# A list scheduler inside the program orders every engine between attention and the last stage; weights are kept as fp32 or as words

## The chip, the cores and the metric

One core of a Trainium2 chip. The time is the device time of one launch, in microseconds; three runs of the kernel before are known, and one execution was recorded by the hardware profiler. PE is the matrix engine; DVE (VectorE), ACT (ScalarE) and POOL (GpSimd) do everything elementwise; SP issues the transfers, all but two small ones at the start.

## The reference

```python
# attention: retention with a decay mask, 4 batches x 8 heads, 576 positions, head width 64
ret = scores * Dmat[None, :, :, :]              # scores = q k^T / sqrt(D), Dmat = gamma^(i-j), lower triangle
x = ret @ v                                     # -> 2304 tokens x 512
# first MLP, 512 -> 2048 -> 512
h = x @ w_in
g = h * np.clip(h + 3.0, 0.0, 6.0) / 6.0
x = g @ w_out
# second MLP, 512 -> 1024 -> 512
h = x @ w_in
e = np.exp(h - h_max)
sm = e / (np.sum(e, axis=-1, keepdims=True) + 1e-09)
solu = h * sm
ln = (solu - mu) / np.sqrt(var + 1e-06) * g_ln
out = ln @ w_out
```

## The kernel before, in words

Every large product is made of three PE passes over numbers split into a high and a low word (hi x hi, hi x lo, lo x hi), so each operand exists as two words: ACT copies the value to the high word, and DVE or POOL subtracts to get the low one. The weights arrive as 64-bit numbers. `Weights.value` (lines 134 to 150) turns half a weight tile, 512 KB, into fp32: ACT reads both 32-bit halves of the raw tile `wraw` (L140, L145), DVE shifts and adds (L148, L149). `wraw`, `wz` and `wt` have two buffers each. `words` (L152) splits the result.

The 2304 tokens are five blocks, 0 to 3 of 512 and 4 of 256. The first MLP has 16 slices of its inner width. After attention come: x2 (the second product) of block 0 over slices 0 to 5 in turns with h (the first product and the gate) of block 1 (`mlp_turns`, L342); h of block 4 and x2 of block 1 over these slices; x2 of block 4. The rest is done by `paired` (L462), which takes two blocks and a list of pairs of slices. For each pair `seven` (L389) makes the seven products of a Strassen-like scheme (a, b, c, d accumulate in four PSUM banks; `plus` adds them, `gate` makes r on ACT and the gated value on DVE), and x2 units of the first block run between the products (`next(units)`). The second block's gated values wait in `later` and are split one by one (`split_g`) while its x2 units run. `paired` is run three times: blocks 0, 1 with pairs 3 to 7; blocks 2, 3 with pairs 0 to 2; blocks 2, 3 with pairs 3 to 7, with `h_4` (L443) for block 4 beside it. The forms of x for `seven` come from `x_sums` (L510), those of the weights from `in_pair` (L196), which converts two halves and makes sums and splits into four `wi` buffers (six there are). `out_half` (L187) converts the second weights, splits them, and stores them to `w1s` in DRAM; `load_out` brings them back. `w2_halves` (L224) does the same for the second MLP's weights.

Conversions stand in one list, `todo` (L891 to 899), taken up by `wq.step()` from hooks at fixed points of the PE's work. Pairs 3 to 7 are in it twice, and pairs 0 to 2 are there although their slices were converted and split in `w1_halves` (L171) during attention.

What sets the order: attention's PE and ACT instructions are kept in program order, and the last stage is pinned wholly (`Pinned`, L60) by a hand-written list of events with times. Between them nothing is pinned: the framework's own timeline model decides, when the program is built, in which order each engine gets its instructions, and also SP its transfers. On the chip each engine and SP's queue then work in that order.

## Time and profile before

| | us |
|---|---|
| median of 3 runs | 729.58 (728.76 to 733.24) |
| the profiled execution | 728.7 |
| its span, first to last instruction | 726.8 |
| PE busy | 662.1 |
| DVE, ACT, POOL busy | 475.5, 421.5, 391.0 |
| mean granted clock of PE, of full speed | 0.948 |

The span counts from the first to the last instruction. PE's busy time also counts the time by which a matmul is longer at the lower of PE's two clock levels (1.2 instead of 2.4 GHz), so it is compared with the time its matmuls need at full clock. The granted clock is an average over a stretch, as a share of full speed. A wait is put down to what released it last.

### The profile page before, as it was taken

The page shows a single profiled execution, that of the slowest core. Times are in us where ns is not written, and L with a number is a line of the kernel's source. Part 1 is how long each engine was busy: PE and PEld are TensorE (multiplying, and loading weights), DVE is VectorE, ACT ScalarE, POOL GpSimd, SP SyncE. Part 2 cuts the span into 40 slices and gives each one's busy share as a digit, 9 for nine tenths or more (in the row PEclk, how much of TensorE's full clock was granted, in tenths as well). Part 3 has the DMA queues.
Part 4 walks back from the last instruction along what each step waited for, and adds up shares of the span by engine and source line. Part 5 has one row for each costly group of instructions (what it writes and reads, how often), then busy time and mean ns, then how long its engine had stood idle before and what let it go on. Part 6 is the DMA issues. An engine that isn't in the chain of part 4 may idle for free.

```text
span 726.8 us, 11418 instructions
## 1 busy us (share of the span) xinstructions
PE 662.1 (91%) x4100; PEld 532.4 (73%) x4100; DVE 475.5 (65%) x791; ACT 421.5 (58%) x736; POOL 391.0 (54%) x372
## 2 busy tenths in 40 slices
PE   9999969989998779968848989979999999999998
PEld 6788848867876458846636878857798888888887
DVE  3766796348889984579335778831138887788760
ACT  5887456556556725356453566543036777777773
POOL 4764553414335766224602343367337989999743
PEclk9999989999999769999985999988999999999999
DMA  9999406887356729733693464796467554443343
GB/s 330 387 357 323 145 28 220 296 282 273 120 158 230 259 68 376 267 120 144 196 380 119 117 205 156 273 367 246 139 186 202 151 94 95 113 103 76 88 93 81
DMA packets 91340, 142.85 MB, mean 197 GB/s; under 512 B 43794, under 2 KB 51090, under 8 KB 91284
## 3 DMA queue, kind: packets, MB, share of 16 engines
q1 hardware_dynamic: 91136, 142.11, 60.4%
q8 instruction: 32, 0.52, 0.3%
q14 instruction: 24, 0.20, 0.1%
q10 hardware_dynamic: 148, 0.02, 0.0%
HBM read 95.18 MB, written 37.49 MB: 183 GB/s over the span
## 4 chain that ended last, share of the span: by engine, by line
PE 51%; DVE 21%; DMA 14%; ACT 7%; issue 6%; POOL 1%; SPq 1%; DVEq 0%; ACTq 0%; POOLq 0%
PE o L68 14%; PE h L68 12%; PE acc L323 10%; DMA wraw<-in_w_dram 9%; DVE wz L149 3%; PE h L300 3%; DVE wz L148 2%; PE xp L569 2%; DVE ws L211 2%; PE s L569 2%; PE x L68 2%; DVE t L401 2%; DVE later L381 2%; DMA wraw<-in_w2i_dram 2%; DMA wraw<-in_w2o_dram 2%
## 5 line engine op out<-in xcount | busy, mean ns | idle before, releaser
L323 PE MATMUL acc<-g,w1l 128*128 128x512 f32 x624 | 170.0, 416 | 24.6 <-ACT g L385 7.9
L323 PEld LDWEIGHTS acc<-g,w1l 128*128 128x128 f32 x624 | 123.2, 202 | 62.6 <-ACT g L385 11.1
L68 PE MATMUL o<-w,lt 128*128 128x512 f32 (+1 forms) x456 | 103.0, 378 | 0.0
L148 DVE TENSOR_SCALAR wz<-wz 128x512 int32<-128x512 int32 x60 | 37.1, 618 | 90.8 <-ACT wz L140 90.7
L68 PEld LDWEIGHTS o<-w,lt 128*128 128x128 f32 x456 | 82.4, 188 | 16.3 <-POOL lt L68 0.4
L386 POOL TENSOR_TENSOR g<-gf,g 128x512 fp32r<-128x512 f32 x26 | 39.6, 1528 | 64.4 <-ACT g L385 63.0
L68 POOL TENSOR_TENSOR lt<-lT,lt 128x512 fp32r<-128x512 f32 x36 | 62.3, 1749 | 15.2 <-ACT lt L68 15.2
L140 ACT ACTIVATE wz<-wraw 128x512 f32<-128x512 f32 x60 | 39.8, 664 | 49.3 <-DMA wraw<-in_w_dram 41.0
L68 ACT ACTIVATE e<-h,stat 128x1024 f32<-128x1024 f32 x36 | 41.3, 1148 | 35.3 <-DVE stat L68 35.3
L149 DVE CUSTOM_DVE_ANT_0 wz<-wz,wt 128x1024 uint16<-128x1024 uint16 x60 | 54.5, 908 | 6.9 <-ACT wt L145 1.8
L219 POOL TENSOR_TENSOR w1f_a<-wz,w1f_a 128x512 fp32r<-128x512 f32 (+1 forms) x26 | 31.3, 1203 | 46.7 <-ACT w1f_a L218 30.8
L300 PE MATMUL h<-x,w 128*128 128x512 f32 (+1 forms) x216 | 49.3, 372 | 7.3 <-DVE gf L313 7.1
L68 PE MATMUL h<-w2t,xt 128*128 128x512 f32 x216 | 53.4, 389 | 0.0
L300 PEld LDWEIGHTS h<-x,w 128*128 128x128 f32 x216 | 36.4, 193 | 17.0 <-DVE gf L313 8.4
L219 POOL TENSOR_TENSOR w1f_s<-ws,w1f_s 128x512 fp32r<-128x512 f32 x13 | 18.2, 1403 | 56.6 <-ACT w1f_s L218 48.6
L386 POOL TENSOR_TENSOR g<-later,g 128x512 fp32r<-128x512 f32 x26 | 38.2, 1488 | 15.4 <-ACT g L385 15.3
L68 PEld LDWEIGHTS h<-w2t,xt 128*128 128x128 f32 x216 | 40.3, 188 | 8.2
L145 ACT ACTIVATE wt<-wraw 128x512 int32<-128x512 uint32 x64 | 42.3, 665 | 0.2 <-POOL w1f_s L219 0.2
L395 PE MATMUL sa<-x_b,w1f_a 128*128 128x512 f32 x96 | 30.9, 456 | 11.4 <-ACT w1f_a L218 8.0
L68 PE MATMUL h<-w2b,xt 128*128 128x512 f32 x162 | 39.7, 390 | 0.0
L317 POOL TENSOR_TENSOR g<-gf,g 128x512 fp32r<-128x512 f32 (+1 forms) x18 | 21.7, 1206 | 33.3 <-ACT g L316 33.2
L380 ACT ACTIVATE r<-t,half 128x512 f32<-128x512 f32 x39 | 28.0, 718 | 17.1 <-DVE t L401 15.5
(180 smaller groups left out, 1448.1 us busy)
## 6 DMA issues: line engine op xcount, KB each, us to landing
wraw<-in_w_dram SPq DMA_DIRECT2D x48, 512.0 KB, 5.9
w1l<-w1s SPq DMA_DIRECT2D x34, 512.0 KB, 6.7
w1s<-w1o SPq DMA_DIRECT2D x10, 512.0 KB, 3.7
rv<-in_vt_dram SPq DMA_DIRECT2D x16, 288.0 KB, 5.6
x2l<-x2s SPq DMA_DIRECT2D x18, 256.0 KB, 4.1
x2f<-x2o SPq DMA_DIRECT2D x18, 256.0 KB, 3.6
x2r<-x2f SPq DMA_DIRECT2D x9, 512.0 KB, 4.3
rq<-in_qt_dram SPq DMA_DIRECT2D x13, 352.0 KB, 6.1
```

Source lines behind the costliest of these rows:

```text
L68: return lambda *args, **kw: self.keep(op(*args, **kw))
L140: first = se.activation(out=z.bitcast(F32), in_=raw[:, :, 1].bitcast(F32), func=ACTF.Prelu, scale=2.0 ** -112, alpha=2.0 ** 32)
L145: second = se.activation(out=t, in_=raw[:, :, 0].bitcast(U32), func=ACTF.Copy, scale=2.0 ** -29)
L148: ve.tensor_scalar(out=z, in0=z, scalar1=3, scalar2=None, op0=ALU.logical_shift_left)
L149: ve.tensor_tensor(out=z, in0=z, in1=t, op=ALU.add)
L219: eng.tensor_tensor(out=w[:, 1, c], in0=src[:, c], in1=f32(w[:, 0, c]), op=ALU.subtract)
L300: mm = nc.tensor.matmul(hp, w1t[ff, 0][:, a, c], xb[t, p][:, b, :n], start=(p == 0 and i == 0), stop=(p == NP - 1 and i == 2),)
L323: te.matmul(acc, w1t[ff, 1][:, a, c], g[:, b], start=(first and i == 0), stop=(last and i == 2))
L380: se.activation(out=r, in_=src, func=ACTF.Relu, scale=1.0 / 6.0, bias=half)
L386: ge.tensor_tensor(out=w[:, 1], in0=src, in1=f32(w[:, 0]), op=ALU.subtract)
L395: te.matmul(bank, forms[k][w][:, a, p * 128:(p + 1) * 128], xf[x][p][:, b], start=(first and p == 0 and i == 0), stop=(last and p == 1 and ...
L569: keep(nc.tensor.matmul(*args, **kw))
```

## The change

From attention's end to the last stage the functions no longer issue instructions. They enter operations into a `Plan`: engine, an assumed duration, what is read and written, and a function that issues it. `place` fixes PE's order as the program has it, gives each buffer's next user the buffers in turn, and works a due time back from PE's ideal times. `run` then goes through time: of the operations ready on an engine it takes the one due first; SP's transfers share a modelled rate; an operation entered with `either` runs on POOL, or on DVE when POOL would be late or DVE is free. The instructions are then issued in that order with all engines pinned. The framework places the waits as before.

Beside it: the words of slices 0 to 5, split during attention, are stored (`w1w`), and pairs 0 to 2 load them and add hi and lo ("words"); pairs 3 to 7 are converted once ("new"), their fp32 values stored in `wf` and loaded for the second time ("kept"). PE's order has other turns: the products of a pair in the order 0, 2, 5, 1, 3, 6, 4; block 4's x2 units in the first pair of the first `paired`, three after each product; the second block's last eight units carried into the next `paired`; x2 opens with two slices on one accumulator. The sums that end banks c and d are written back to PSUM. Of `t` there are three buffers instead of four, of `x2l` four instead of two; the pool of attention is released at once. The last stage is the same.

```diff
+    HOP, DMA_US, DMA_KB, DMA_ONE = 0.2, 2.2, 330.0, 150.0
...
+    def op(self, engine, us, fn, reads=(), writes=(), kb=0, slack=0.0, alt=None):
+        o = Op(len(self.ops), engine, us, fn, kb, slack, alt)
...
+        for key in (*reads, *writes):
+            for k in self.related(key):
+                w, r = self.last.setdefault(k, ([], []))
+                o.after.update(w)
+                if key in writes:
+                    o.after.update(r)
+        for key in (*reads, *writes):
+            self.last[key][key not in writes].append(o)
...
+    def lag(self, a, b):
+        same = 0.0 if a.engine == "PE" else 0.03
+        return b.slack + (same if a.engine == b.engine and a.engine != "SP" else self.HOP)
+
+    def length(self, o):
+        return self.DMA_US + o.kb / self.DMA_ONE if o.engine == "SP" else o.us
...
+
+        pe = [o for o in self.ops if o.engine == "PE"]
+        now, ideal = 0.0, {}
+        for a, b in zip(pe, pe[1:]):
+            b.after.add(a)
+        for o in pe:
+            ideal[o] = now
+            now += o.us
...
+                if len(slots) >= bufs:
+                    kept = all(any(o.engine == "PE" for o in v.ops) for v, _ in slots)
+                    free = min(range(len(slots)), key=lambda i: slots[i][1]) if kept else 0
+                    old = slots.pop(free)[0]
+                    b.ops[0].after.update(old.ops)
+                    assert b.ops[0] not in old.ops, (b.name, old.name)
+                if first:
+                    b.ops[0].begun.add(first)
+                first = b.ops[0]
+                slots.append((b, max(asap[o] + self.length(o) for o in b.ops)))
+        order = self.sorted_ops()
...
+            if o in ideal:
+                due = min(due, ideal[o] + o.us)
+            o.due = min(o.due, due - self.length(o))
+            for v in o.begun:
+                v.due = min(v.due, o.due)
...
+                waiting[o.engine].append(o)
+        dma, done = 0.0, []
+
+        def late(o, t):
+            busy = sum(v.us for v in waiting["POOL"] if v.due < o.due and ready[v] <= t)
+            return max(free["POOL"], t) + busy > o.due
+
...
+            if e == "DVE":
+                urgent = [v for v in spare if late(v, begin[e])]
+                mine = mine + urgent or [v for v in spare if free["POOL"] > begin[e]]
...
+            if e == "SP" and dma > begin[e] + 2.0:
+                mine = [v for v in mine if v.due < begin[e] + 30.0]
+                if not mine:
+                    free["SP"] = min([dma - 1.9, *(ready[v] for v in waiting["SP"] if ready[v] > begin[e])])
+                    continue
+            o = min(mine, key=lambda v: (v.due, v.at))
+            soon = [ready[v] for v in waiting[e] if begin[e] < ready[v] < begin[e] + 0.8 and v.due < min(o.due - 10.0, ready[v] + 8.0)]
+            if soon and e != "SP" and e != "PE":
+                free[e] = min(soon)
+                continue
+            waiting[o.engine].remove(o)
+            if o.engine != e:
+                o.engine, o.us = o.alt
+            o.start = begin[e]
+            if e == "SP":
+                free[e] = o.start + 0.1
+                dma = max(dma, o.start) + o.kb / self.DMA_KB
+                o.end = max(dma, o.start + o.kb / self.DMA_ONE) + self.DMA_US
+            else:
+                free[e] = o.end = o.start + o.us
+            done.append(o)
+            for v, t in [(v, o.end + self.lag(o, v)) for v in nexts[o]] + [(v, o.start) for v in starts[o]]:
+                ready[v] = max(ready[v], t)
...
+    def move(kb, fn, r, w, store=False):
+        return pl.op("SP", 0.1, fn, r, w, kb=kb, slack=0.8 if store else 0.0)
+
+    A_US, V_US, S_US, L_US = 0.66, 0.7, 0.97, 1.5
...
+    def raw_of(src):
+        b = buf("wraw", [128, 512, 2], "wraw", I32)
+        move(512, lambda: sy.dma_start(out=b().rearrange("p n t -> p (n t)"), in_=src), (), (b,))
+        return b
...
+    def either(us, other, fn, r, w):
+        o = pl.op("POOL", other, lambda: fn(ve if o.engine == "DVE" else ge), r, w, alt=("DVE", us))
...
+    def store_of(b, dst, key, kb=512):
+        move(kb, lambda: sy.dma_start(out=dst, in_=f32(b())), (b,), (key,), store=True)
+
+    def out_first(ff, z):
+        w = WK[ff, 1] = buf("wo", WIDE, f"w1_{ff}_1", F32R)
+        words_of(w, z)
+        store_of(w, w1s[ff], ("w1s", ff))
+
+    def out_later(ff):
+        raw = raw_of(w1[ff][:, 1024:])
+        w = buf("ws", WIDE, f"w1o{ff}", F32R)
+        words_of(w, value_of(raw))
...
+    def in_pair(k, how):
...
+        if how == "words":
+            f = []
+            for i, names in enumerate((("a11", "a12"), ("a21", "a22"))):
+                w = buf("wi", WIDE, f"w1f{k}_{names[0]}", F32R)
+                move(512, lambda w=w, i=i: sy.dma_start(out=f32(w()), in_=w1w[2 * k + i]), (("w1w", 2 * k + i),), (w,))
+                forms[k].update({n: (w, at) for n, at in zip(names, (lo, hi))})
+                z = buf("wz", W, "wz", I32)
+                either(S_US, L_US, lambda e, w=w, z=z: e.tensor_tensor(
+                    out=z().bitcast(F32), in0=f32(w()[:, 0]), in1=f32(w()[:, 1]), op=ALU.add), (w,), (z,))
+                f.append((z, lambda z=z: z().bitcast(F32)))
+        elif how == "kept":
+            raw = buf("wraw", [128, 512, 2], "wraw", I32)
+            view = lambda: raw().rearrange("p n t -> p (n t)").bitcast(F32).rearrange("p (i n) -> p i n", i=2)
+            move(512, lambda: sy.dma_start(out=view(), in_=wf[k]), (("wf", k, 0), ("wf", k, 1)), (raw,))
+            f = [(raw, lambda: view()[:, 0]), (raw, lambda: view()[:, 1])]
+        else:
+            f = [value_of(raw_of(w1[2 * k + i][:, :1024])) for i in range(2)]
+            f = [(z, lambda z=z: z().bitcast(F32)) for z in f]
+            for i, (z, v) in enumerate(f):
+                move(256, lambda i=i, v=v: sy.dma_start(out=wf[k][:, i], in_=v()), (z,), (("wf", k, i),), store=True)
+        (f1, v1), (f2, v2) = f
+        s12, s34 = (buf("wt", W, f"{n}_{k}") for n in ("ws12", "ws34"))
+        for out, a, b, r, w, op in (
...
+                out=out(), in0=a(), in1=b(), op=op), (*r, w) if w in r else r, (w,))
+        if how != "words":
+            form(("a11", "a12"), v1, f1)
+        form(("s1", "s2"), s12, s12)
+        form(("s3", "s4"), s34, s34)
+        if how != "words":
+            form(("a21", "a22"), v2, f2, slice(0, 512) if how == "kept" else hi)
+
...
+        acc = [pl.buf((ps_c, "h2", 2), WIDE, F32, f"acc{t}_{ffs[0]}_{i}") for i in range(2 // share)]
+        last, begun = len(ffs) - 1, set()
+        order = [(k, d) for ds in ((0, 1), (2, 3)) for k in range(2) for d in ds] if ends > 1 else []
+        order += [(k, d) for k in range(len(order) // NP, last + 1 - ends) for d in range(NP)]
+        for k, d in order + [(k, d) for d in range(NP) for k in range(last + 1 - ends, last + 1)]:
...
+        def step(p):
+            if p == 0:
+                bk["a"] = a = bank(f"sa{t}_{k}", at=0)
+                product(a, "a11", "b11", True, False)
+                on_act(A_US, lambda: se.activation(out=u2(), in_=a(), func=ACTF.Copy), (a,), (u2,))
+            elif p == 2:
...
+            elif p == 1:
+                product(bk["a"], "a12", "b21", False, True)
+                gated(2 * k, bk["a"])
+            elif p == 6:
+                product(bk["c"], "a22", "t4", False, True)
+                plus(bk["c"], bk["c"], u2)
+                gated(2 * k + 1, bk["c"])
...
+    def paired(ta, tb, ks, xf, evac, carry, per=1, with_4=False, keep_out=False):
+
+        ffs = [2 * k + i for k in ks for i in range(2)]
+        later = {}
+        units = x2_units(ta, ffs, evac)
+        for n, k in enumerate(ks):
+            later[k] = buf("wbo" if 0 < n < 4 else "g2", WIDE, f"later{tb}_{k}")
+            order = (0, 2, 5, 1, 3, 6, 4) if n < len(ks) - 1 else (0, 2, 5, 1, 6, 3, 4)
+            for j, _ in enumerate(seven(ta, k, xf, later[k], order)):
+                for _ in range(per + (j == 5) if n == 0 else 1 + (j == 5) if n < len(ks) - 1 else (0, 1, 0, 1, 1, 2, 0)[j]):
+                    next(units if n else carry, None)
...
+        held = ks[-3:]
+        order = [2 * k + i for k in (*held, *ks[-4::-1]) for i in range(2)]
...
+        for i, _ in enumerate(units):
+            yield "b", i
+        rest = x2_units(tb, order, evac, ready)
+        for i in range(4 * len(order) - (0 if with_4 else 8)):
+            next(rest)
+            yield "c", i
+        carried.append(rest)
...
-    w2q = w2_halves(pb)
-    todo = []
-    for item in (
-        [out_half(ff) for ff in FB[:6]], in_pair(3, False), in_pair(4, False), in_pair(5, False), [out_half(FB[6])],
-        in_pair(6, False), [out_half(FB[7])], in_pair(7, False), [out_half(FB[8])], [out_half(FB[9])], w2q[:4],
-        in_pair(0, False), in_pair(1, False), w2q[4:5], in_pair(2, False), w2q[5:11], in_pair(3, True),
-        *(x for k, j in zip(pairs_b[1:], range(11, 15)) for x in (in_pair(k, True), w2q[j:j + 1])), w2q[15:],
-    ):
-        todo += item
...
+    for ff in FIRST:
+        store_of(WK[ff, 0], w1w[ff], ("w1w", ff))
+    out_first(FIRST[1], known("wz", wq.begun[0]))
+    out_first(FIRST[2], value_of(known("wraw", wq.raws[8])))
+    for ff in FIRST[3:]:
+        out_first(ff, value_of(raw_of(w1[ff][:, 1024:])))
+    for i, _ in enumerate(x2_units(0, FIRST, evac_partial, ends=1)):
+        if i % NP == NP - 1:
+            h_of(1, FIRST[i // NP])
+    slots_4 = iter(["x2l"] * 4 + ["xraw"] * 2)
+    for ff in FIRST:
+        h_of(4, ff, next(slots_4))
+    for _ in x2_units(1, FIRST, evac_partial):
         pass
...
+    carried = [x2_units(4, FIRST, evac_partial)]
+    for ff in FB[:6]:
+        out_later(ff)
+    in_pair(3, "new")
+    in_pair(4, "new")
+    early_forms()
+    in_pair(5, "new")
+    for k in (6, 7):
+        out_later(FB[k])
+        in_pair(k, "new")
+    out_later(FB[8])
+    out_later(FB[9])
+    for d in range(NP):
...
+    in_pair(0, "words")
+    in_pair(1, "words")
+    for n in range(2):
+        w2_half(n)
+    in_pair(2, "words")
+    for n in range(2, 4):
+        w2_half(n)
+    in_pair(3, "kept")
+    for n in range(4, 6):
+        w2_half(n)
+    for _ in paired(2, 3, pairs_a, xforms[2], evac_partial, carried.pop()):
         pass
...
+    for o in pl.run({"ACT": 2.0, "DVE": 2.0, "POOL": 2.0, "SP": 2.0}):
+        o.fn()
...
```

## Rows read from the trace of the kernel before

**Rows 1.** Windows: stages A to D and the last; busy us (instructions) by engine
```profile
83.13:155.08 71.95, 64.84 (x338) 54.94 (x336) 45.50 (x55) 38.27 (x72) 30.07 (x23) 0.95 0.59 189
155.08:283.20 128.12, 110.59 (x427) 84.03 (x427) 104.44 (x134) 74.49 (x134) 66.70 (x46) 0.89 0.61 210
283.20:373.40 90.20, 76.26 (x307) 58.51 (x305) 53.72 (x78) 44.45 (x76) 32.85 (x25) 0.96 0.63 222
373.40:524.76 151.36, 130.97 (x570) 104.96 (x571) 83.04 (x120) 69.49 (x118) 64.84 (x52) 0.89 0.61 212
...
562.00:694.00 132.00, 132.00 (x584) 109.31 (x583) 104.71 (x200) 97.35 (x152) 115.88 (x116) 1.00 0.46 106
```
**Rows 2.** The chain in order of time: start, us, what
```profile
283.84 2.72 PE acc L323 x12
...
529.10 2.15 PE x L68 x18
```
**Rows 3.** PE in order of time, after gaps of 0.71 and 8.01 us
```profile
175.66 1.20 PE L395 MATMUL sb<-x_t,w1f_s 128*128 128x512 f32 x4 [0.71 <-DVE w1f_s L219]
...
381.37 3.43 PE L395 MATMUL sa<-x_b,w1f_a 128*128 128x512 f32 x6 [8.01 <-ACT w1f_a L218]
```
**Rows 4.** Waits of PE: us in total, times, longest (seven of 18)
```profile
PE sa L395 <- ACT w1f_a L218: 10.2, 2, 8.0
PE acc L323 <- ACT g L385: 7.9, 6, 2.2
PE h L300 <- DVE gf L313: 7.1, 2, 6.4
PE sb L395 <- ACT w1f_s L218: 7.1, 3, 4.3
PE acc L323 <- POOL g L386: 6.5, 5, 3.1
PE acc L323 <- DVE x2o L804: 6.3, 6, 1.7
PE acc L323 <- ACT x2p L542: 3.8, 4, 1.2
```
**Rows 5.** The chain between 92 and 147 us
```profile
92.81 2.32 DVE xs_n L514
...
136.55 0.66 ACT wt L145
...
138.77 1.37 DVE w1o L159
...
140.16 0.32 SPq L192
...
140.53 6.29 DMA wraw<-in_w_dram
```
**Rows 6.** ACT by line and shape, 83 to 525 us: count, busy, mean ns
```profile
L145 ACT ACTIVATE wt<-wraw 128x512 int32<-128x512 uint32 x56 | 36.9, 663 | 0.2 <-POOL w1f_s L219 0.2
```
**Rows 7.** DVE by line and shape, 83 to 525 us
```profile
L149 DVE CUSTOM_DVE_ANT_0 wz<-wz,wt 128x1024 uint16<-128x1024 uint16 x53 | 49.6, 936 | 5.8 <-ACT wt L145 0.9
L148 DVE TENSOR_SCALAR wz<-wz 128x512 int32<-128x512 int32 x53 | 34.1, 643 | 86.2 <-ACT wz L140 86.1
...
L401 DVE TENSOR_TENSOR t<-sc,t 128x512 f32<-128x512 f32 x26 | 17.8, 685 | 2.5 <-PE sc L395 2.1
...
L507 DVE TENSOR_TENSOR x_t<-xl_b,x_t 128x512 fp32r<-128x512 f32 x4 | 5.3, 1343 | 0.0
...
L507 DVE TENSOR_TENSOR x_t<-xs_b,x_t 128x512 fp32r<-128x512 f32 x4 | 2.6, 678 | 0.0
```
**Rows 8.** POOL by line and shape, 83 to 525 us
```profile
L386 POOL TENSOR_TENSOR g<-gf,g 128x512 fp32r<-128x512 f32 x26 | 39.6, 1528 | 64.4 <-ACT g L385 63.0 <-PE acc L323 1.3
...
L867 POOL TENSOR_TENSOR xt<-s,xt 128x512 fp32r<-128x512 f32 x2 | 2.5, 1272 | 0.0
```
**Rows 9.** The page's head
```profile
span 726.8 us, 11418 instructions
```

More of the change, by code (lines that the diff above doesn't have):

```diff
@@ L87, in mm_tile @@
         return ps_mm[side].tile(shape, F32, tag="mm", name=name)
+    w1w = [dram.tile([128, 2, 512], F32, name=f"w1w{ff}") for ff in range(FA)]
+    wf = [dram.tile([128, 2, 512], F32, name=f"wf{k}") for k in range(NFF // 2)]
     xd = dram.tile([128, NP, 1024], F32, name="xd")
@@ L443, in h_4 @@
-    def h_4(k):
-        h = mm_tile([128, 512], f"h4_{k}", 1)
-        for i in range(2):
-            for p in range(NP):
-                w = forms[k][("a11", "a12", "a21", "a22")[2 * i + p // 2]]
-                for j, (a, b) in enumerate(((0, 0), (0, 1), (1, 0))):
-                    te.matmul(
-                        h[:, 256 * i:256 * i + 256], w[:, a, (p % 2) * 128:(p % 2) * 128 + 128], xb[4, p][:, b],
-                        start=(p == 0 and j == 0), stop=(p == NP - 1 and j == 2),
-                    )
-        gf = p0.tile([128, 512], F32, tag="gf", bufs=2, name=f"gf4_{k}")
-        gate(h, gf, f"4_{k}")
-        nc.sync.dma_start(out=g4s[k], in_=gf)
@@ new lines, in h_4, with go @@
+    def h_4(k):
+        h = bank(f"h4_{k}", at=1)
+        def go():
+            for i in range(2):
+                for p in range(NP):
+                    w, at = forms[k][("a11", "a12", "a21", "a22")[2 * i + p // 2]]
+                    for j, (a, b) in enumerate(((0, 0), (0, 1), (1, 0))):
+                        te.matmul(
+                            h()[:, 256 * i:256 * i + 256], w()[:, a, at][:, (p % 2) * 128:(p % 2) * 128 + 128],
+                            XK[4, p]()[:, b], start=(p == 0 and j == 0), stop=(p == NP - 1 and j == 2),
+                        )
+        pl.op("PE", 24 * 0.12, go, (*(forms[k][n][0] for n in ("a11", "a21")), *(XK[4, p] for p in range(NP))), (h,))
+        gf = buf("gf", W, f"gf4_{k}")
+        gate_of(h, (h,), gf, (gf,), f"4_{k}")
+        move(256, lambda: sy.dma_start(out=g4s[k], in_=gf()), (gf,), (("g4s", k),), store=True)
@@ new lines, in retention_hardswish_solu_kernel @@
+    for k in pairs_b[1:]:
+        for n in range(2):
+            w2_half(2 * k - 2 + n)
+        in_pair(k, "kept")
+    w2_half(14)
+    w2_half(15)
+    for d in range(NP):
+        load_part(2, d)
+    XT = [buf("x", WIDE, f"xt{k}", F32R) for k in range(NX)]
+    g4, G4 = {}, {}
+    def load_g4(i):
+        gf = buf("r", W, f"gf4l_{i}")
+        move(256, lambda: sy.dma_start(out=gf(), in_=g4s[pairs_b[i]]), (("g4s", pairs_b[i]),), (gf,))
+        h = G4[i] = XT[7] if i == 4 else buf("g2", WIDE, f"g4_{i}", F32R)
+        split(lambda: (h()[:, 0], h()[:, 1]), gf, (gf,), (h,))
@@ new lines, in first_x2, with go, first_forms, step @@
+    def first_x2(i):
+        b = buf("ws", [128, NP, 256], f"x2r{i}")
+        def go():
+            x2r[i] = b()[:, :2], b()[:, 2:]
+            sy.dma_start(out=b(), in_=x2f[0][:, :, 256 * i:256 * i + 256])
+        move(512, go, [("x2f", 0, d) for d in range(NP)], (b,))
+        return b
+    def first_forms(b):
+        s = [buf("xraw", [128, 2, 2, 128], f"{n}_0") for n in ("s12", "s34")]
+        made = []
+        def step(k):
+            if not made:
+                xt.extend(v() for v in XT)
+                made.extend(chain(*forms_x2(0, [v() for v in s])))
+            made[k]()
+        for k, v, r in ((0, 0, ()), (1, 0, (s[0],)), (2, 1, ()), (3, 1, (s[0], s[1]))):
+            on_ge(0.8, lambda k=k: step(k), (b, *r), (s[v],))
+        for k, x, src in ((0, 3, b), (1, 0, b), (2, 1, s[0]), (3, 2, s[1])):
+            us = 0.5 if k == 0 else 1.0
+            on_act(0.65 * us, lambda k=k: step(4 + k), (src,), (XT[x],))
+            on_ge(L_US * us, lambda k=k: step(8 + k), (src, XT[x]), (XT[x],))
@@ L998, in product, with load_x2p @@
+    def load_x2p(t, k):
+        n = BLOCKS[t][1]
+        if k * 512 < NP * n:
+            part = pb.tile([128, 512], F32, tag="x2l", bufs=4, name=f"x2l{t}_{k}")
+            part = part.rearrange("p (d n) -> p d n", n=n)
+            share = 512 // n
+            sy.dma_start(out=part, in_=x2s[t][:, k * share:(k + 1) * share])
+            parts[k] = part
+            for d in range(share):
+                x2p[t, k * share + d] = part[:, d]
     def product(i, p):
```

810 lines of the change are left out of this document (435 added, 375 removed).

## The prediction

> **What bounds the kernel now.** I read the windows by stage first, then the chain, then what the PE waited for, then the shapes of the other engines' work. The execution is three parts: attention to 83 us, a middle to 524.76 us (end of the last unit before the last stage's first matmul), and a last stage. In the last stage PE is busy for 132.0 of 132.0 us at a granted clock of 1.00 [rows 1], under an order written by hand: nothing is to be had there, and the change leaves it alone. The middle is four stages: A (x2 of blocks 0 and 1, h of 1 and 4), B (blocks 0, 1 with pairs 3 to 7), C (blocks 2, 3 with pairs 0 to 2), D (blocks 2, 3 with pairs 3 to 7).
>
> What must the PE do in the middle? From the loops: 840 x2 matmuls (72 of them 256 wide), 13 pairs x 42 = 546, h of block 1 with 60 still to do, h of block 4 72 narrow ones, h_4 120 narrow ones: 1374 wide and 264 narrow (1638; the windows count 1642 [rows 1]). At full clock twelve wide ones take 2.72 us and eighteen narrow ones 2.15 us [rows 2], so 0.2267 and 0.1194 us each: 311.5 + 31.5 = 343.0 us. By stage 62.0, 95.5, 69.6, 116.3 (343.4; roundings). The four stages last 441.6 us and PE is busy 382.7 in them [rows 1]: 59.0 us idle, and 39.3 us more busy time than the matmuls need. That second loss is the clock, 0.89 to 0.96 there: six matmuls after an 8.01 us gap took 3.43 us, four after a 0.71 us gap only 1.20 [rows 3]. So 98.2 us lie between now and a PE that never stops, at 0.67 us of slow clock for each idle microsecond.
>
> Where the 59.0 us go [rows 4]: (a) weight forms of a pair late, 17.3; (b) splits of g late, 14.4; (c) an accumulator not yet evacuated, 10.1; (d) a gate of h late, 7.1; (e) the rest, 10.1, mostly small waits inside `seven`. Behind (a) stands the ring of two `wraw` buffers, and the order of SP's queue. The chain shows one round [rows 5]: ACT has read a buffer at 137.21, but the next load is issued at 140.53, because the store of the w1o (L192), made at 140.14 by DVE, stands ahead of it; then the load takes 6.3 us. Every weight half of 512 KB goes through this ring.
>
> **The change part by part.** *Conversions removed.* Pairs 3 to 7 are converted twice now (10 halves) and pairs 0 to 2 again after `w1_halves` (6 halves). Sixteen conversions go, each two reads of 0.663 us on ACT and 0.643 + 0.936 on DVE [rows 6, 7]: 21.2 us of ACT, 25.3 of DVE. Added: six sums hi + lo (0.68 to 1.34 us on DVE, 1.5 on POOL [rows 7, 8]; I take 1.5: 9 us), and for pairs 0 to 2 the splits of a11 and a21 go, about 3 x (1.5 + 0.9) = 7 us. DVE and POOL together are busy 286.7 + 194.5 = 481 us in A to D [rows 1]; they come to about 458, of two engines. All of it stands off the path unless late, hidden under PE's products, so its direct worth is nil; were DVE the bound it would be the 25 us. Its worth is in D: of 21 raw loads in D's pairs ten become five, and those need no conversion.
>
> The last sums of c and d are now written back to PSUM instead of to `t`, 26 of them. No row shows that; the nearest, 0.685 from PSUM to SBUF, says no change, the blocked 1.34 is the upper bound [rows 7] (17 us of DVE, most of it under PE): I take 0.
>
> *Transfers.* Sixteen loads of 0.524 MB go (8.4 MB); six stores and six loads of words (6.3 MB), ten stores and five loads of fp32 (5.2 MB) come: +3 MB, 11 DMAs more, SP's issue about 0.32 us each [rows 5]: 3.5 us, spread. A to D move 92.6 MB now (GB/s x time); at 210 GB/s for a share of 0.61 [rows 1] the full rate would be some 344 GB/s, so 95.6 MB need 278 us: less than any forecast here. The last 33 us of D are the exception (14 loads for the last stage, 4 of w1l, g4 and x2r: 11 MB, 32 us at that rate); I put 3 us there (f), bounds 0 and 8.
>
> *The order.* (d): DVE made the x sums, from 92.8 on [rows 5], ahead of a gate; ordered by due time the gate goes first, and the sums are wanted only by B: 0 left. What is late next is pair 3 itself. PE reaches it after 204 wide and 72 narrow matmuls, 54.8 us after 83.1: 138. Its second half is the 12th conversion. At 6.3 us for a load [rows 5] and 1.33 of ACT two buffers give one every 3.8 us: from 85 to 131, plus some 6 us of DVE, ACT and POOL for value, sums and splits: 137, just in time. With the 3.3 us behind a store in each round it is one every 5.5: 157, 19 late. So (a) keeps 0 to 19 there; I take 5, as the plan sets stores behind their data, and nothing for C and D, where words and kept fp32 need no conversion ahead of the pair. (c): x2_units now opens with two accumulating halves, so the second bank is wanted after 2.72 us instead of 1.36, and an evacuation by DVE is about 0.69, as its other sums from PSUM [rows 7]: 2 left. (b): only five units of the first block go out in the last pair, so eleven cover its last gates, and the split may run on DVE; but the g buffers still come free only as units end: half, 7 left. (e): the steps of `seven` are the same and the engines beside it denser: 12.
>
> Sum of idle left: 5 + 7 + 2 + 0 + 12 + 3 = 29. Of the slow clock: five gaps alone, the longest of their kinds, make 24 of the 59, and three of these, 18.7, belong to (a) and (d) [rows 4]; shorter ones cost less clock [rows 3]; I take 0.3 us per idle microsecond (bounds 0 and the 0.67 of now): 9. Left 38 of 98.2, so 60 us gained: A 67, B 110, C 76, D 129.
>
> The profiled execution took 728.7 us with a span of 726.8 [rows 9]; 728.7 - 60 = 669. The median of the runs, 729.58, is 0.9 above it, inside their spread.
>
> **A resource that the plan does not see.** POOL's subtraction takes 1.27 us at its shortest and 1.53 on average; DVE's sum of two SBUF tensors takes 0.68 or 1.34 and more, while the DVE sums with one operand in PSUM stay at 0.685 [rows 7, 8]. DVE and POOL hold each other up, on these shapes alone. The plan prices both at fixed averages (0.97 and 1.5) as if independent. The Trainium skill (SBUF — State Buffer, Who interferes with whom) says that a DVE instruction with two SBUF inputs and a GpSimd instruction that reads SBUF exclude each other, the second waiting until the first has finished; the two durations agree. By the rows alone, in B, the tightest: some 77 splits and sums that either engine can take, 20 conversions. With 60% on DVE: 46 x 0.68 + 31 x 1.27 + 20 x 1.58 = 102 us of work that takes turns, against B's 95.5 of PE. So B cannot well come to its PE minimum, and 110 is near what it can do. Were the exclusion complete, as that page has it, B's floor would be this 102 instead of 95.5; the forecast for B lies above both.
>
> **Rivals.** *PE-bound middle* (0.17): the order works as in the last stage; only (e) is left, 12 with no slow clock: 728.7 - 98.2 + 12 = 643 (638 to 650). For it: the last stage. Against: B's exclusion. *The exclusion decides* (0.20): the 117 steps of `seven` that read PSUM (nine a pair) each come 0.4 us later behind a held-up op (between 0 and 0.66, what x_t has over its 0.68 [rows 7]): 47 us, of which the unit between two products hides half; 23 more, 31 with the clock: 700 (690 to 717). *Stalls elsewhere take it all back* (0.05): within 1%, 722 to 737. *Slower* (0.13): SP's queue, now fixed wholly by the plan. One load behind a store that is late costs 3.3 us [rows 5], 5.5 with the slow clock of now. 44 loads go through the ring; from 19 of them late (105 / 5.5) the kernel is slower by over 1%; at two a pair, 26: 728.7 - 98.2 + 143 = 773. Against: the plan puts a store 0.8 us after its data, and issues by due time (loads of one ring in the order written); for: its DMA time is a model.
>
> **How the numbers follow.** The forecast holds 0.45 (650 to 690). Faster by over 1%: 0.17 + 0.45 + 0.20 = 0.82; within 1% (about what a measurement of this kernel can tell from no change) 0.05; slower 0.13. The range 638 to 717 leaves out the last two.
>
> **What would show it.** Middle near 382 us, by stage as above; clock 0.97 or more; `sa` and `sb` waiting on forms under 6 us, h on gf none; ACT reading wraw 48 times a word instead of 64; POOL's busy share of the middle up from 44%. Wrong: SP waits of several us ahead of wraw loads, DVE steps of `seven` on the chain, or PE idle for over 2 us at the start of B or of the last stage.

## The result: 648 us, and the profile after

The median is 648.05 us (four runs, 647.36 to 648.7) against 729.18 for the kernel before run beside it: a ratio of 0.887, 95% interval 0.884 to 0.890. The profiled execution took 648.7 us with a span of 647.0, PE is busy for 627.4 of them (97%) and its mean granted clock is 0.997 instead of 0.948. The gain is 81 us. The time stands inside the predicted range (638 to 717), 21 us below the predicted 669 and inside the bounds of the rival that was called a PE-bound middle.

Windows of the kernel after, as in [rows 1]: stretch, its length, busy us and (x instructions) of PE, PEld, DVE, ACT and POOL, granted clock, DMA share, GB/s. The first four are the stages A to D, the last one the last stage.

```profile
80.65:148.83 68.18, 59.90 (x289) 50.16 (x288) 54.69 (x58) 43.05 (x82) 48.73 (x33) 0.97 0.82 279
148.83:256.00 107.17, 106.22 (x501) 88.82 (x500) 85.42 (x104) 62.42 (x112) 69.78 (x55) 1.00 0.75 251
256.00:318.40 62.40, 61.71 (x272) 50.52 (x271) 37.66 (x49) 33.56 (x57) 50.88 (x41) 1.00 0.60 209
318.40:444.90 126.50, 123.36 (x596) 103.14 (x595) 74.41 (x99) 67.78 (x115) 76.20 (x63) 1.00 0.84 295
...
481.00:613.00 132.00, 132.00 (x584) 109.28 (x584) 104.68 (x200) 96.72 (x149) 115.88 (x116) 1.00 0.46 108
```

The middle lasts 364.25 us (80.65 to 444.9) where it lasted 441.6. PE is idle in it for 364.25 - 351.19 = 13.1 us instead of 59.0. At full clock its matmuls need the 343.4 us of before and 2.7 more, because twelve wide matmuls of h of block 1, which stood in attention, now stand in the middle (12 x 0.2267): 346.1. So 5.1 us are left of the 39.3 that went to the slower clock. Attention ends 2.5 us earlier, about those same twelve; the last part is as it was (647.0 - 444.9 = 202.1 against 202.0). The 2.5 and the middle's 77.4 us are, to 0.1, the whole difference of the two spans, 79.8. The stages can't be set side by side one for one. Block 4's x2 moved from A to B (60 of its 72 matmuls; twelve stood there before). Eight units of three matmuls run over from B into C and eight from C into D; before, twelve ran over from B into C and none from C into D. The instruction counts fit this to within three.

What PE waited for in the middle after (releaser; us in total, times, longest), to be read against [rows 4]:

```profile
PE h L68 <- DVE gf L68: 4.4, 2, 3.0
PE acc L68 <- DVE x2o L68: 3.1, 4, 0.8
PE acc L68 <- ACT x2p L68: 2.3, 4, 0.7
PE acc L68 <- DVE w L68: 2.1, 1, 2.1
PE acc L68 <- DVE xa L576: 1.1, 1, 1.1
```

These are all of the 13.1 but for rounding. No product of `seven` waits for a form, a split of g or a step of `seven`.

### The profile page after: what moved, and what is told of

The parts are those of the page before. It is cut to its first block, busy times and chain, and to the rows that moved or that the text cites. A ratio compares the mean times of both kernels' runs of the same rounds, so it can differ in the third digit from the quotient of the medians.

```text
span 647.0 us, 11379 instructions
## 1 busy us (share of the span) xinstructions
PE 627.4 (97%) x4100; PEld 519.9 (80%) x4100; DVE 439.2 (68%) x711; ACT 400.3 (62%) x698; POOL 444.3 (69%) x420
## 4 chain that ended last, share of the span: by engine, by line
PE 88%; DVE 5%; DMA 3%; ACT 2%; issue 1%; SPq 0%; DVEq 0%; ACTq 0%
PE acc L68 26%; PE h L68 16%; PE o L68 15%; PE sd L68 5%; PE sa L68 5%; PE sc L68 5%; DVE wz L68 3%; PE h L400 3%; PE sb L68 3%; PE xp L449 3%; PE x L68 2%; PE s L449 2%; DMA wraw<-in_w_dram 1%; PE u L449 1%; DMA xd<-xa 1%
## 5 line engine op out<-in xcount | busy, mean ns | idle before, releaser
L68 PE MATMUL acc<-g,w1l 128*128 128x512 f32 x624 | 156.0, 391 | 3.8 <-DVE x2o L68 3.1
L68 POOL TENSOR_TENSOR g<-gf,g 128x512 fp32r<-128x512 f32 (+1 forms) x31 | 43.4, 1401 | 37.5 <-ACT g L68 36.5
L68 PE MATMUL acc<-g,w 128*128 128x512 f32 (+1 forms) x216 | 44.8, 357 | 4.9 <-DVE w L68 2.1
L68 PEld LDWEIGHTS acc<-g,w 128*128 128x128 f32 x216 | 36.3, 189 | 12.5 <-DVE w L68 2.5
L68 DVE CUSTOM_DVE_ANT_0 wz<-wz,wt 128x1024 uint16<-128x1024 uint16 x36 | 41.3, 1153 | 2.2 <-ACT wt L68 0.4
L68 PEld LDWEIGHTS h<-w2b,xt 128*128 128x128 f32 x162 | 30.2, 188 | 6.1
L68 DVE SCALAR_TENSOR_TENSOR h<-h,e 128x1024 f32<-128x1024 f32 x18 | 31.2, 1735 | 5.5 <-ACT e L68 5.3
L68 DVE TENSOR_SCALAR e<-h,stat 128x1024 f32<-128x1024 f32 x18 | 20.6, 1142 | 21.0 <-POOL stat L68 21.0
L68 DVE CUSTOM_DVE_ANT_0 h<-h,h 128x512 f32<-128x512 f32 x36 | 24.7, 685 | 13.2 <-ACT h L68 6.5
L68 PE MATMUL h<-x,w 128*128 128x512 f32 (+1 forms) x144 | 27.8, 350 | 4.4 <-DVE gf L68 4.4
```

Of the source, the lines that this page charges most:

```text
L68: return lambda *args, **kw: self.keep(op(*args, **kw))
```

## The experiments

Each run is compared with runs of the kernel before beside it on the same chip, whose medians lie between 729.18 and 734.45; so the ratios are what is compared. One thousandth is 0.73 us.

| kernel | median us | ratio (95%) | clock |
|---|---|---|---|
| after | 648.05 | 0.887 (0.884 to 0.890) | 0.997 |
| e1 conversions twice | 665.92 | 0.907 (0.903 to 0.911) | 0.985 |
| e2 nothing pinned | 663.43 | 0.904 (0.899 to 0.909) | 0.990 |
| e3 by text, not by due time | 656.04 | 0.895 (0.890 to 0.900) | 0.997 |
| e4 all on POOL | 677.36 | 0.924 (0.919 to 0.928) | 0.985 |
| e5 fixed engines | 645.54 | 0.881 (0.878 to 0.884) | 0.997 |
| e6 PE's turns of before | 668.77 | 0.912 (0.909 to 0.915) | 0.989 |
| e7 all of e1, e2, e3, e5, e6 | 670.75 | 0.916 (0.912 to 0.919) | 0.985 |
| e8 two PE waits taken away | 648.59 | 0.886 (0.883 to 0.889) | 0.992 |
| e9 e7 and the old hooks | 687.19 | 0.937 (0.933 to 0.941) | 0.978 |
| e10 e7 and the old rings | 676.78 | 0.922 (0.919 to 0.926) | 0.985 |
| e11 after, fast loads in the plan | 702.99 | 0.959 (0.955 to 0.962) | 0.968 |
| e12 before, three raw buffers | 698.34 | 0.953 (0.949 to 0.956) | 0.973 |

### e1: the conversions put back

```diff
-    for ff in FIRST:
-        store_of(WK[ff, 0], w1w[ff], ("w1w", ff))
...
-        if how == "words":
+        if how == "never":
...
-        elif how == "kept":
+        elif how == "never":
...
-            for i, (z, v) in enumerate(f):
+            for i, (z, v) in ():
```

> The changed kernel, but pairs 0 to 2 and the second use of pairs 3 to 7 convert their weights from the 64-bit numbers again: 16 conversions more (each 2 x 0.66 us on ACT, 0.64 + 0.94 us on DVE as the trace of before has them), no w1w and no wf in DRAM. Theory A (the order made the gain, the removed conversions were only cover): 648 to 658 us, and the middle keeps a granted clock of 0.98 or more. Theory B (less work for ACT and DVE made it): at least half of the 81 us comes back, 685 us or more.

Measured: 20 thousandths slower than after, about 15 us, between the two forecasts. ACT reads 56 raw words in the middle again (40 in after). The largest single loss in PE's timeline stands at the first pair of D:

```profile
353.38 1.22 PE L68 MATMUL sb<-x_t,w1f_s 128*128 128x512 f32 x2 [5.75 <-ACT w1f_s L68]
```

It is not the whole loss, as e1's windows of C and D show (62.40 and 126.50 us in after):

```profile
258.52:327.41 68.89, 63.63 (x272) 51.58 (x271) 50.35 (x69) 43.84 (x77) 45.45 (x39) 0.98 0.69 234
327.41:461.86 134.45, 125.41 (x596) 103.94 (x595) 81.44 (x117) 72.88 (x124) 69.03 (x57) 0.97 0.80 280
```

C loses 6.5 us and D 8.0. So the kept weights and words are worth something, half of it in D, where the prediction put their worth, and nearly half in C; most of the gain is not theirs.

### e2 and e3: nothing pinned; the first in the text instead of the first due

```diff
-    ve, se, ge, te, sy = (Pinned(tc, e) for e in (ve, se, ge, te, sy))
```

> The changed kernel with the same plan, issued in the same sequence, but the engines of the middle are not pinned: the framework's timeline model orders each engine's instructions again. Theory A (the plan's order): much of the gain is lost, 680 to 730 us, with idle gaps of 2 us and more before products again. Theory C (what counts is the work and the turns in which the program gives PE its products, and any order of the other engines does): 648 to 660 us.

```diff
-            o = min(mine, key=lambda v: (v.due, v.at))
+            o = min(mine, key=lambda v: v.at)
```

> The changed kernel, pinned, but the plan takes on each engine and on SP, of the operations that are ready, the one that stands first in the program instead of the one due first. PE's order is the same. Theory A in its narrow form (due times matter): x sums and conversions go ahead of gates again, 665 to 710 us. If being ready decides and due times do not: 646 to 652 us.

Measured: 17 and 8 thousandths, some 12 and 6 us. With the plan's sequence as its input, the framework's own choice of order costs 12 us, just above the lower of its forecasts; taking whichever ready operation stands first in the text costs 6, between its forecasts. Neither pinning nor due times is the main thing.

### e4 and e5: who does the splits and sums

```diff
-        o = pl.op("POOL", other, lambda: fn(ve if o.engine == "DVE" else ge), r, w, alt=("DVE", us))
+        o = pl.op("POOL", other, lambda: fn(ve if o.engine == "DVE" else ge), r, w)
```

> The changed kernel, but every split and sum that either engine may take goes to POOL. By the counts of the prediction some 223 units of 1.27 us (alone) to 1.53 us (held up) and 8 us more: 290 to 350 us of POOL in a middle of 364. Theory D (DVE and POOL hold each other up, so the sharing is what keeps B near PE's pace): POOL is late in B and A, 665 to 700 us. Rival (the sharing matters little, since DVE is then less held up): 648 to 655 us.

Measured: 37 thousandths, inside the forecast of theory D; it shows that POOL is then full, not that the two engines hold each other up. In the whole run PE waits 10.5 us, in eleven gaps, for forms that POOL makes. 1.7 us of them stand in the window below (columns as above), of which POOL is busy 85%:

```profile
150.00:270.00 120.00, 109.25 (x480) 87.82 (x479) 55.16 (x75) 62.14 (x110) 102.18 (x85) 0.96 0.68 223
```

In e5 every such operation has a fixed engine, as in the kernel before:

```diff
-    def either(us, other, fn, r, w):
-        o = pl.op("POOL", other, lambda: fn(ve if o.engine == "DVE" else ge), r, w, alt=("DVE", us))
+    def either(us, other, fn, r, w, on="POOL"):
+        if on == "DVE":
+            on_ve(us, lambda: fn(ve), r, w)
+        else:
+            on_ge(other, lambda: fn(ge), r, w)
```

> One part undone: every split and sum that the plan may give to POOL or DVE has a fixed engine again, as in the kernel before (every third weight split on POOL, sums on DVE, splits of g and of h on POOL). Order, due times, pinning, kept weights and PE's turns stay. Theory E (the free choice of engine is itself worth something, because it goes to whichever of the two is idle): 658 to 675 us, with PE waits on g splits or on weight forms of several us. Theory F (any sensible sharing does, as long as the order by due time stays; the kernel with everything on POOL lost only because POOL was full there): 646 to 652.

Measured: 0.881, and nothing was lost: 645.54 is just under the forecast of theory F, and the intervals of e5 and after just touch, with e5 the faster. DVE and POOL together are busy 271.3 + 185.0 = 456 us in e5's middle, 252.2 + 245.6 = 498 in that of after. So the free choice of engine is no part of the gain.

### e6: PE's turns of before

```diff
-        order = [(k, d) for ds in ((0, 1), (2, 3)) for k in range(2) for d in ds] if ends > 1 else []
+        order, ends = [], 2
...
-            order = (0, 2, 5, 1, 3, 6, 4) if n < len(ks) - 1 else (0, 2, 5, 1, 6, 3, 4)
+            order = (0, 2, 5, 3, 1, 6, 4)
...
-                for _ in range(per + (j == 5) if n == 0 else 1 + (j == 5) if n < len(ks) - 1 else (0, 1, 0, 1, 1, 2, 0)[j]):
+                for _ in range(0 if n == 0 else 1 + (j == 6)):
```

> One part undone: PE's turns are those of before (products of a pair in the order 0, 2, 5, 3, 1, 6, 4; x2 does not open with two slices on one accumulator; no units carried from one call of paired to the next, so the first pair of a call has no units between its products and the second block's units all go out at the end). The plan, its due times, the pinning, the sharing and the kept weights stay. Theory G (the list scheduler does the work and PE's turns are a detail): 648 to 656. Theory H (without units between the products of the first pair, and with waits for an accumulator at each opening of x2, PE waits again): 660 to 685, the waits being sc on gf or acc on x2p and x2o.

Measured: 25 thousandths, some 18 us. PE's longest waits in e6 are the accumulators that were forecast, 12.4 us in 16 short gaps, where after has 5.4 in eight:

```profile
PE acc L68 <- ACT x2p L68: 6.3, 9, 1.2
PE acc L68 <- DVE x2o L68: 6.1, 7, 1.4
```

### e7: all of it undone at once

The edits of e1, e2, e3, e5 and e6 together.

> All parts that were undone one by one go back together: conversions twice, fixed engines, PE's turns of before, ready operations taken in program order, nothing pinned between attention and the last stage. What is left of the change is the plan's buffers and its sequence of issue, and the sums of c and d in PSUM. If the parts add up and nothing else in the change is worth anything: 715 to 735 us, as before. If something that was not taken apart (the buffer rings by the plan, the sums in PSUM) carries some of the gain: 685 to 705.

Measured: 0.916, and both forecasts are wrong. One by one the five cost 20 + 17 + 8 - 6 + 25 = 64 thousandths; together 29. They don't add. A likely reason, which no run isolates, is that a kernel in which PE already waits for an accumulator has room for a late form. And 84 thousandths, 62 us, remain with every part gone but the plan itself and its buffers. PE's waits in e7:

```profile
PE acc L948 <- DVE x2o L923: 6.3, 4, 3.5
PE acc L948 <- ACT w L737: 6.2, 1, 6.2
PE sd L971 <- DVE u L980: 3.7, 1, 3.7
```

Weights are converted twice, and still no form of a pair is waited for; before, these waits were 17.3 us [rows 4].

### e8: two of the last waits taken away

The h of block 4 are put between the units of x2 of block 1, and two neighbouring columns of an accumulator no longer follow one another at the end:

```diff
-    for ff in FIRST:
-        h_of(4, ff, next(slots_4))
-    for _ in x2_units(1, FIRST, evac_partial):
-        pass
+    for i, _ in enumerate(x2_units(1, FIRST, evac_partial)):
+        if i % 2 and i // 2 < FA:
+            h_of(4, FIRST[i // 2], next(slots_4))
...
-        for k, d in order + [(k, d) for d in range(NP) for k in range(last + 1 - ends, last + 1)]:
+        for k, d in order + [(k, d) for d in ((0, 2, 1, 3) if share == 1 else range(NP)) for k in range(last + 1 - ends, last + 1)]:
```

> A try at the waits that are left in the kernel after. The six h of block 4, which stand back to back there (4.4 us of PE waiting on gf), are put between the units of x2 of block 1, and the last four columns of the x2 of the last call go in the order 0, 2, 1, 3, so that two neighbours no longer share one two-bank accumulator tile (3.1 us of PE waiting on x2o, in steps of 0.78). If these waits are real and stand on the path, since PE has no other idle time: 648 minus 5 to 8, so 640 to 644. If PE only meets them elsewhere (the plan is laid out anew, or the next ring is the limit): 646 to 650.

Measured: no gain, as the second forecast has it. The wait for gf is gone, the four gaps of 0.8 us on x2o are down to one of 1.8, and another stands where x2 of block 1 now begins, before the accumulators of block 0 are read:

```profile
120.09 2.93 PE L68 MATMUL acc<-g,w 128*128 128x512 f32 x6 [5.74 <-ACT x2p L68]
```

### e9 and e10: the hooks, and the rings

```diff
+    for i, made in enumerate(items):
+        for o in made:
...
+                if i:
+                    o.after.add(points[i - 1])
+            else:
+                o.after.add(points[i])
```

> All parts go back as in the run with everything undone (670.75 us, 62 under the kernel before), and beside them each of the 52 conversions is tied again to the point of PE's work at which the kernel before takes it up (its hook): the raw load not before the hook ahead of its own, the rest not before its hook, in the order of the old list. Theory I (what is left of the gain is that conversions no longer wait for a fixed point of PE's work but start as soon as their buffers are free): 700 to 735 us, with PE waiting 10 us or more for forms of w1f in sa, sb or sc. Theory J (the hooks stood early enough; what counts is that a ready instruction is never queued behind one that is not ready, on SP above all, where loads no longer stand behind stores): 665 to 685, form waits under 5 us.

```diff
-    PB = {"wbi": 4, "wbo": 4, "g2": 4, "t": 3, "xraw": 2, "ws": 2, "x2l": 4}
+    PB = {"wbi": 4, "wbo": 4, "g2": 4, "t": 4, "xraw": 2, "ws": 2, "x2l": 2}
...
-                plus(bk["c"], bk["c"], u2)
-                gated(2 * k + 1, bk["c"])
+                u4 = buf("t", W, f"u4_{t}_{k}")
+                plus(u4, bk["c"], u2)
+                gated(2 * k + 1, u4)
...
-                plus(bk["d"], bk["d"], u2)
-                kept_gate(0, bk["d"], True)
+                plus(u2, bk["d"], u2)
+                kept_gate(0, u2, False)
```

> The run with everything undone, and beside it the last differences in data: four buffers of t and two of x2l as before, g of block 4 in t, the sums that end banks c and d written to SBUF instead of back to PSUM. Theory K (rings and PSUM sums carry some of the 62 us that are left): 680 to 700. Theory L (they carry nothing; the order alone does): 668 to 676.

Measured against e7: the hooks cost 21 thousandths (15 us), the rings and the sums in PSUM 7 (5 us). Both lie between their two forecasts, nearer the lower (687.19 against 665 to 685, 676.78 against 668 to 676). In e9 the wait for a form of a pair is 2.9 us and 0.6, not 10: the hooks explain a quarter of what was left, and not by the wait that was forecast for them. The two edits were not tried together.

### e11: the same plan with a wrong price for transfers

What, then, does the plan's order have that the order before lacked? Waits of DVE and ACT in the kernel before, from 83 to 525 us:

```profile
DVE wz L148 <- ACT wz L140: 86.1, 31, 13.1
...
ACT wz L140 <- DMA wraw<-in_w_dram: 41.0, 15, 6.7
```

DVE stands 31 times, up to 13.1 us, at the shift of a raw word that ACT has not read. ACT in its turn stands 15 times at a load of this kind that has not landed. In after the first row reads so:

```profile
DVE wz L68 <- ACT wz L68: 9.8, 8, 3.1
```

The plan believes that a load of 512 KB lands 2.2 + 512 / 150 = 5.6 us after its issue; after's profile has 5.5 for the median of 32. In e11 it believes 1.0:

```diff
-    HOP, DMA_US, DMA_KB, DMA_ONE = 0.2, 2.2, 330.0, 150.0
+    HOP, DMA_US, DMA_KB, DMA_ONE = 0.2, 0.5, 2000.0, 1000.0
```

> The kernel after, unchanged but for the plan's price of a transfer: 0.5 us + 1 us per 1000 KB and 2000 KB per us for the queue, instead of 2.2 us + 1 us per 150 KB and 330 KB per us. So the plan believes that a 512 KB load lands after 1.0 us (5.6 before), and sets conversions and loads of x2 too early in the order of ACT and DVE. In the kernel before DVE stands 86.1 us (31 times, longest 13.1) at the shift of a raw word that ACT has not read yet, with other work queued behind it; in the kernel after 9.8, and in the run with everything undone 21.0. Theory M (what the order is worth is that no engine stands at an instruction whose load has not landed): DVE at wz back at 30 us or more, 665 to 700 us. Theory N (the buffers decide when a conversion can come, and due times keep it behind urgent work anyway; the model of transfers is a detail): 646 to 655.

Measured: 72 thousandths slower than after, 52 us, more than any other single edit, and just above the forecast of 665 to 700; DVE at wz is 27.1 us, a little under what was forecast. It is ACT that stands: 54.6 us at raw loads of all three kinds (of w, w2i and w2o), where after has 6.9. The costliest place, in e11's timeline (start, us, engine, what; in brackets the idle time before it and what ended it):

```profile
352.43 0.66 ACT L68 ACTIVATE wt<-wraw 128x512 int32<-128x512 uint32 x1 [17.39 <-DMA wraw<-in_w2i_dram]
...
353.51 0.58 ACT L68 ACTIVATE u<-sa 128x512 f32<-128x512 f32 x1
...
355.56 0.59 ACT L68 ACTIVATE x2p<-acc 128x512 f32<-128x512 f32 x1
...
354.12 0.69 DVE L68 TENSOR_TENSOR u<-sb,u 128x512 f32<-128x512 f32 x1 [27.69 <-ACT u L68]
...
356.20 1.65 PE L68 MATMUL acc<-g,w1l 128*128 128x512 f32 x3 [9.14 <-ACT x2p L68]
```

ACT stands 17.39 us at a conversion for the second MLP, whose products begin only when the middle has ended. The load it stands at was issued at 344.25. Behind it in ACT's queue are the copy of `sa`, for which DVE stands 27.69 us, and the evacuation for which PE stands 9.14. These 9.14 are what the place costs; `sa`'s product itself ended only at 342.98, so the first part of the long waits cost nothing. The Trainium skill (PSUM — Partial Sum Buffer, Engine vs sequencer instructions) says that the queues of ScalarE, VectorE and GpSimd are strictly first in, first out. The rows agree: the copy of `sa`, whose product had ended, began only behind the conversion, at 353.51.

### e12: the kernel before with a third raw buffer

```diff
-AHEAD = 2
-WRAW = 2
+AHEAD = 3
+WRAW = 3
```

> The kernel before with three raw buffers instead of two and loads asked for three steps ahead instead of two, nothing else. Theory M (before, ACT and DVE stand at conversions because raw loads come late, 6 us each behind two buffers and stores): the 86.1 us of DVE at wz fall under 40, the waits for forms of w1f (17.3) mostly go, and the time falls to 695 to 715. Theory O (the order of the instructions loses the time, wherever the loads are): 722 to 737, DVE at wz still over 60.

Measured: 0.953, some 35 us from two constants, inside the forecast of the first theory; the second falls. PE's wait for a form shrinks from 17.3 us [rows 4] to the first of these rows and 0.3 more. ACT's wait for a raw load of w falls from 41.0 to 13.3. DVE still stands 57.8 us, more than the 40 that were forecast:

```profile
PE sb L395 <- ACT w1f_s L218: 2.2, 2, 2.0
...
PE h L300 <- DVE gf L313: 7.0, 2, 6.4
...
DVE wz L148 <- ACT wz L140: 57.8, 25, 20.0
...
ACT wz L140 <- DMA wraw<-in_w_dram: 13.3, 9, 4.3
```

So the sum of DVE's standing doesn't measure the cost; what is queued behind it, and when that is wanted, must count as well. The gate of h, late behind the x sums, is untouched (7.0 us here, 7.1 in [rows 4]): that part of the loss is order alone.

## Why the prediction was right, and where it was off

**What bounds the kernel.** Right. The change was worth what PE's idle time and the clock behind it were worth: 98.2 us could be had, 80.1 of the middle's loss were (59.0 - 13.1 and 39.3 - 5.1), nearly nothing elsewhere.

**The sum.** It left 29 idle and 9 of slow clock; 13.1 and 5.1 were left. These 19.8 us are nearly the whole miss of 21. None of the six idle terms came near its own size: (c) and (d) were too low, the others too high, and 1.1 us at the start of A stand in no term. By its terms:

- (a) weight forms, 5: none in a pair; 2.1 for one word of the second weights in A.
- (b) splits of g, 7: 0. The g buffers that "come free only as units end" held nothing up.
- (c) accumulators, 2: 3.1 + 2.3 = 5.4, on both kinds. The four on x2o stand where the second half of a two-bank accumulator is written right after its first half was finished; that the reading of the one holds up the other is inferred from their place, and e8 speaks for it.
- (d) gates of h, 0: 4.4, but not the gate that was meant. The six h of block 4 stand back to back, 1.4 us of matmuls each, and the gate did not keep that pace.
- (e) small waits inside `seven`, 12: 0. This is the term that was mis-sized most. "The same steps beside denser engines" held for the engines, not for PE. PE's turns alone don't explain it: a unit of x2 now stands between any two products that depend on each other, but with the turns of before (e6) such waits are still only 1.3 us, while without pinning (e2) they are 4.2 and with all undone (e7) 8.9. The runs point to the order of the other engines.
- (f) transfers at the end of D, 3: 0, at 295 GB/s over all of D.
- Slow clock, 0.3 us for each idle microsecond: 5.1 / 13.1 = 0.39, between the bounds.

**Conversions.** ACT's reads fell by 16 (56 to 40 in the middle, [rows 6]) as said, and e1 sizes their worth with the rest in place: 15 us, 8.0 of it in D as said and 6.5 in C, where the prediction put none. "Direct worth nil" was too low as a statement on the whole kernel. DVE and POOL were to be busy 458 us and were 498. That number was right for the work, as e5 has 456 with fixed engines; what came on top came with the free choice. It gives POOL 190 operations and DVE 309, where e5 has 135 and 363, and POOL takes longer for each; and the conversion's two rows on DVE take 12.5 us longer than in e5 (rows below).

**The exclusion of DVE and POOL.** The mechanism was there, and its consequence was not. B, of which the text said that it could not well come to PE's minimum, lasts 107.17 us with PE busy 106.22. But this B is no test of the floor of 102: with block 4's x2 moved in, its own PE minimum is 105.2 (426 wide and 72 narrow matmuls), already above the floor, and 14 conversions stand in it where the sum counted 20. DVE's durations did rise: by shape in the middle (count, busy, mean ns) the two rows of the conversion that stand at 936 and 643 in [rows 7] are in after, and then in e5

```profile
L68 DVE CUSTOM_DVE_ANT_0 wz<-wz,wt 128x1024 uint16<-128x1024 uint16 x36 | 41.3, 1153 | 2.2 <-ACT wt L68 0.4
L68 DVE TENSOR_SCALAR wz<-wz 128x512 int32<-128x512 int32 x36 | 29.7, 827 | 10.0 <-ACT wz L68 9.8
...
L68 DVE CUSTOM_DVE_ANT_0 wz<-wz,wt 128x1024 uint16<-128x1024 uint16 x36 | 35.3, 980 | 1.7
L68 DVE TENSOR_SCALAR wz<-wz 128x512 int32<-128x512 int32 x36 | 23.2, 646 | 4.0 <-ACT wz L68 4.0
```

e5 is as dense as after (its middle lasts 362 us) and has nearly the durations of before: the rise belongs to the free choice of engine, not to the denser order.

The rival that gave 700 needed nine steps of each pair to come 0.4 us later on PE's path. They may have come later; PE waited for none of them. It reached 0.20 of the chance on durations alone, without asking what stood beside the step.

**The rivals.** The PE-bound middle (643, bounds 638 to 650) describes the result better than the forecast of 669, and it was set aside for the exclusion. 648.05 lies outside the forecast's own 650 to 690, to which 0.45 was given, and inside this rival's bounds, to which 0.17 was; the range held because it took the rival in. The slower case, SP's queue, did not come: in the middle before, SP stood 96 us in 15 waits for words still to be stored, in its four longest rows of that kind; no wait for a form of a pair is left in after. Yet the sign that was to show it, SP waits of several us ahead of `wraw` loads, did come, with no loss to PE:

```profile
SPq L68 <- ACT wt L68: 48.3, 23, 6.8
```

SP stands there until ACT has freed a raw buffer. Of the other signs, the clock (0.997), the waits of `sa` and `sb` (0), ACT's 48 reads and POOL's share (67%) came as said; h on gf, which was to be none, is 4.4. The rival's condition was the right one to name, as e11 shows: much hangs on the plan's model of a transfer, and with a wrong price for it 72 of the 113 thousandths go.

**What the prediction did not see.** It costed the order as the sum of waits that end. The runs name a mechanism behind them: a conversion at the head of an engine's queue whose load has not landed, with urgent work behind it. e11 brings it back and costs 52 us, though its wrong price reorders SP's transfers as well; e12 asks for the loads earlier and gains 35. ACT stands at raw loads for 52.6 us in the middle before, 54.6 in e11, 30.8 in e12, 25.6 in e7 and 6.9 in after; in before and in e7 mostly in these rows:

```profile
ACT wz L140 <- DMA wraw<-in_w_dram: 41.0, 15, 6.7
...
ACT wt L719 <- DMA wraw<-in_w_dram: 14.5, 12, 3.1
```

This standing alone does not put the runs in order: e9 has 24.1 us of it and is slower than e7. That e7's 62 us come from conversions set later in the queue is therefore argued, not shown: 15 of them go with the hooks (e9) and 5 with the buffers and the sums in PSUM (e10). What is left open: how the 63 thousandths between e9 and the kernel before divide between SP's order, the buffers, and the order of ACT and DVE was not taken apart.

## What to carry to other kernels

When several engines wait in turn, look in the trace for an engine that stands at an instruction whose load has not landed and ask what is queued behind it; one more buffer and one more step ahead were worth 35 us here, where the whole rewritten schedule gave 81. A scheduler that runs ahead of time hangs on its price for a transfer, so take that price from the profile (here 5.6 us against 5.5 measured; with 1.0 instead, 52 of the 81 us were lost). Parts of a change that each cost something when undone need not add up: undo them together as well.

## What the runs showed of the hardware that was not expected

DVE and POOL hold each other up on single instructions, in both directions, and PE need not notice. After's timeline, POOL and DVE at two places:

```profile
202.84 1.29 POOL L68 TENSOR_TENSOR w1f_a<-wz,w1f_a 128x512 fp32r<-128x512 f32 x1 [1.80 <-ACT w1f_a L68]
...
202.88 1.80 DVE L68 CUSTOM_DVE_ANT_0 wz<-wz,wt 128x1024 uint16<-128x1024 uint16 x1
204.60 0.68 DVE L68 TENSOR_TENSOR u<-sb,u 128x512 f32<-128x512 f32 x1
...
205.76 0.68 DVE L68 TENSOR_TENSOR u<-sc,u 128x512 f32<-128x512 f32 x1
...
209.26 0.68 DVE L68 TENSOR_TENSOR w1f_s<-ws,w1f_s 128x512 fp32r<-128x512 f32 x1
...
209.28 1.26 POOL L68 TENSOR_TENSOR w1f_a<-wz,w1f_a 128x256 fp32r<-128x256 f32 x1
```

At the first place POOL began 0.04 us ahead and ended at 204.13; DVE's sum of two SBUF tensors, 0.69 alone at 366.10 in the kernel before, took 1.80, to 204.68. The two sums with one operand in PSUM took 0.68 with POOL at work beside them (until 205.56, and from 205.64 to 206.44). At the second place DVE began 0.02 us ahead, and POOL took 1.26 for half a tile; its sums of that size take 0.74 to 0.80 elsewhere in this stretch. By the rule that the prediction cited from the Trainium skill (SBUF — State Buffer, Who interferes with whom) the second of such a pair waits until the first has finished. 204.13 + 0.69 would be 204.82, and the trace agrees to 0.14 us.
